# Layer 2 by one level of Strassen (7 products), remainder tokens as one 512-token group, batch 0 by head halves, loads on GpSimd's queue, and an issue order from a list scheduler

## The chip, the cores and the metric

One core of one Trainium2 chip. The metric is the device time of one execution in microseconds (us), the median of several; the span of a profile is a little shorter than that time. Engines are named as in the profile: PE is TensorE (matmul), DVE is VectorE, ACT is ScalarE, POOL is GpSimd, SP is SyncE, which here only issues DMAs.

## The reference, cut to what matters

```python
# q, k, v: (8 batches, 8 heads, 576 tokens, 64), float32
def attn(q, k, v):
    phi = lambda x: concat([relu(x) * cos_w, relu(x) * sin_w], axis=-1)   # 128 features
    q_p, k_p = phi(q), phi(k)
    kv  = einsum('bhsf,bhsd->bhfd', k_p, v)
    z   = sum(k_p, axis=2)
    num = einsum('bhsf,bhfd->bhsd', q_p, kv)
    den = einsum('bhsf,bhf->bhs', q_p, z)[..., None] + 1e-6
    return num / den

x   = attn(q, k, v).transpose(0, 2, 1, 3).reshape(4608, 512)
h   = x @ w_in                 # layer 1: 512 -> 2048
out = (h * cos(h)) @ w_out     # layer 2: 2048 -> 512
```

A batch has 576 = 4 x 128 + 64 tokens. Four tiles of 128 are its own; the 64 left over, the remainder, pair with the 64 of the next batch into a fifth tile.

## The kernel before

The parts that the change and the argument touch. All loads of q, k, v and all transposing DMAs are issued by SP, in one queue:

```python
    def load(b, name, after=None):
        ...
        m, n = raw[name], b % 2                      # one f32 buffer each for q, k, v
        five, four = tokens(srcs[name][b])
        nc.sync.dma_start(out=blocks(m, n), in_=five)
        nc.sync.dma_start(out=blocks(m, 1 - n)[:, :, 0:NT, :], in_=four)

    def q_trans_dma(b):                              # batches 2 to 7; PE transposes 0 and 1
        nc.sync.dma_start_transpose(
            out=qTs[b].rearrange("f t h p -> f (t h) p"),
            in_=qps[b].rearrange("p t h g d -> p (t h g d)"))

    def num(b, t):
        ... # matmuls of qT with kvz, then on DVE: den, reciprocal, x16 = N * rec
            if b >= NPE:
                nc.sync.dma_start_transpose(out=x_dst(b, t), in_=x16s[(b, t)])

    def moe1(b, j, s0=0, s1=SM):                     # layer 1: 4 matmuls of 512 columns
        ...
        gate(gts[b][:, j, s0:s1], M1)                # ACT: sin(h + pi/2); DVE: product

    def moe2(key, t, gsl, j0=0, j1=NJT):             # layer 2: 16 matmuls of 512 columns
        ...
            nc.tensor.matmul(
                M2, lhsT=gts[key][:, j, gsl], rhs=w_out_sb[:, j, :],
                start=(j == 0), stop=(j == NJT - 1))
```

The next batch's attention is spread by hand over the layers of the present one.

Of the kernel before, what the change touches and what calls it, by code (L numbers as in the profile page):

```python
# [13 lines left out]
F16 = mybir.dt.float16  # L14


@with_exitstack
def kernel(
# [31 lines left out]
    for n in range(2):  # L50
# [11 lines left out]
        tc.tile_pool(name="ppool", bufs=8, space=bass.MemoryType.PSUM))  # L62
# [5 lines left out]
    V1 = [cpool.tile([P, NT + 1, H, D1], F16, name=f"V1_{n}") for n in range(2)]  # L68

    srcs = {"k": k, "v": v, "q": q}  # L70
    raw = {nm: cpool.tile([P, H, NT + 1, D], F32, name=f"{nm}m") for nm in srcs}
    kvzs, kps, qps, qTs, x16s, xts, gts, m2s, osts = {}, {}, {}, {}, {}, {}, {}, {}, {}
    ALLP = slice(0, P)


    late = []

    def flush():
        todo, late[:] = list(late), []
        for f in todo:  # L80
            f()

    def tokens(ap):

        return (ap[..., 0:S5, :].rearrange("h (p t) d -> p h t d", t=NT + 1),
                ap[..., S5:S, :].rearrange("h (p t) d -> p h t d", t=NT))

    def load(b, name, after=None):
        if b >= B:
            return  # L90
        m, n = raw[name], b % 2
        if after is not None:
            nc.gpsimd.tensor_copy(out=m[0:2, 0, 0, 0:1], in_=after)
        five, four = tokens(srcs[name][b])
        nc.sync.dma_start(out=blocks(m, n), in_=five)
        nc.sync.dma_start(out=blocks(m, 1 - n)[:, :, 0:NT, :], in_=four)

    def feat(b, name, t, g, act):


        dst = (kps if name == "k" else qps)[b][:, t, :, g, :]
        src, sc = raw[name][:, :, t, :], CS[:, b % 2, g, t:t + 1]
        if act:
            nc.scalar.activation(out=dst, in_=src, func=AF.Relu, scale=sc)  # L104
        else:
            nc.vector.tensor_scalar(  # L106
                out=dst, in0=src, scalar1=0.0, scalar2=sc, op0=ALU.max, op1=ALU.mult)

    def val(b, t, act):
        dst, src = V1[b % 2][:, t, :, 0:D], raw["v"][:, :, t, :]  # L110
        if act:
            nc.scalar.activation(out=dst, in_=src, func=AF.Copy)  # L112
        else:
            nc.vector.tensor_copy(out=dst, in_=src)  # L114

    def kv_group(b, hb):
        KV = ppool.tile([P, HB, D1], F32, name=f"KV{b}_{hb}", tag="ps")
        for hh in range(HB):
            h = hb * HB + hh
            for t in range(NT + 1):  # L120
                nc.tensor.matmul(  # L121
                    KV[:, hh, :], lhsT=kps[b][:, t, h].rearrange("p g d -> p (g d)"),
                    rhs=V1[b % 2][:, t, h, :], start=(t == 0), stop=(t == NT))
        nc.scalar.activation(
            out=kvzs[b][:, hb * HB:(hb + 1) * HB, :], in_=KV, func=AF.Copy)

    def q_trans_dma(b):

        nc.sync.dma_start_transpose(
            out=qTs[b].rearrange("f t h p -> f (t h) p"),  # L130
            in_=qps[b].rearrange("p t h g d -> p (t h g d)"))

    def q_trans(b, t):
        QP = ppool.tile([P, H, P], F16, name=f"QP{b}_{t}", tag="ps")
        for h in range(H):
            nc.tensor.matmul(  # L136
                QP[:, h, :], lhsT=qps[b][:, t, h].rearrange("p g d -> p (g d)"),
                rhs=IDENT, is_transpose=True)
        nc.scalar.activation(out=qTs[b][:, t], in_=QP, func=AF.Copy)  # L139

    def num(b, t):

        parts = [b - 1, b] if t == NT else [b]
        N = [ppool.tile([P, HB, D1], F32, name=f"NUM{b}_{t}_{hb}", tag="ps")
             for hb in range(2)]
        for hb in range(2):
            for hh in range(HB):
                h = hb * HB + hh
                for n, p in enumerate(parts):
                    nc.tensor.matmul(  # L150
                        N[hb][:, hh, :], lhsT=qTs[p][:, t, h, :], rhs=kvzs[p][:, h, :],
                        start=(n == 0), stop=(n == len(parts) - 1))

        def ratio():
            den = apool.tile([P, H], F32, name=f"den{b}_{t}", tag="den")
            for hb in range(2):
                nc.vector.tensor_scalar_add(
                    out=den[:, hb * HB:(hb + 1) * HB], in0=N[hb][:, :, D], scalar1=1e-6)
            rec = apool.tile([P, H], F32, name=f"rec{b}_{t}", tag="rec")
            nc.vector.reciprocal(out=rec, in_=den)  # L160
            x16 = apool.tile([P, H, D], F16, name=f"x16{b}_{t}", tag="x16", bufs=4)
            for hb in range(2):
                sl = slice(hb * HB, (hb + 1) * HB)
                nc.vector.tensor_tensor(
                    out=x16[:, sl, :], in0=N[hb][:, :, 0:D],
                    in1=rec[:, sl].unsqueeze(2).broadcast_to((P, HB, D)), op=ALU.mult)
            x16s[(b, t)] = x16.rearrange("p h d -> p (h d)")
            if b >= NPE:
                nc.sync.dma_start_transpose(out=x_dst(b, t), in_=x16s[(b, t)])
        late.append(ratio)  # L170

    def x_dst(b, t):
        if t < NT:
            return xts[b][:, :, t * P:(t + 1) * P]
        xts[("r", b // 2)] = apool.tile([P, NCT, P], F16, name=f"xTr{b}", tag="xTr")
        return xts[("r", b // 2)]

    def x_trans(b, t):
        XP = ppool.tile([P, NCT, P], F16, name=f"XP{b}_{t}", tag="ps")
        for c in range(NCT):  # L180
            nc.tensor.matmul(
                XP[:, c, :], lhsT=x16s[(b, t)][:, c * P:(c + 1) * P], rhs=IDENT,
                is_transpose=True)
        nc.scalar.activation(out=x_dst(b, t), in_=XP, func=AF.Copy)

    def attention_tiles(b):
        kps[b] = apool.tile([P, NT + 1, H, 2, D], F16, name=f"kp{b}", tag="kp", bufs=1)
        qps[b] = apool.tile([P, NT + 1, H, 2, D], F16, name=f"qp{b}", tag="qp", bufs=1)
        kvzs[b] = apool.tile([P, H, D1], F16, name=f"kvz{b}", tag="kvz", bufs=3)
        qTs[b] = apool.tile([P, NT + 1, H, P], F16, name=f"qT{b}", tag="qT")  # L190
        xts[b] = apool.tile([P, NCT, SM], F16, name=f"xT{b}", tag="xT")

    def gate(dst, M1):

        n = M1.shape[-1]
        ch = apool.tile([P, SM], F32, name="ch", tag="ch", bufs=4)
        nc.scalar.activation(out=ch[:, 0:n], in_=M1, func=AF.Sin, bias=PIH, scale=1.0)  # L197
        flush()
        late.append(lambda: nc.vector.tensor_tensor(
            out=dst, in0=M1, in1=ch[:, 0:n], op=ALU.mult))  # L200

    def moe1(b, j, s0=0, s1=SM):
        if b not in gts:
            gts[b] = gpool.tile([P, NJT, SM], F16, name=f"g{b}", tag="g")
        M1 = ppool.tile([P, s1 - s0], F32, name="M1", tag="ps")
        for c in range(NCT):
            nc.tensor.matmul(  # L207
                M1, lhsT=w_in_sb[:, c, j * P:(j + 1) * P], rhs=xts[b][:, c, s0:s1],
                start=(c == 0), stop=(c == NCT - 1))
        gate(gts[b][:, j, s0:s1], M1)  # L210

    def moe1_rem(pr, jg):
        if jg == 0:
            gts[("r", pr)] = gpool.tile([P, NJT, P], F16, name=f"gr{pr}", tag="gr")
        M1 = ppool.tile([P, 4, P], F32, name="M1", tag="ps")
        for jj in range(4):
            j = jg * 4 + jj
            for c in range(NCT):
                nc.tensor.matmul(  # L219
                    M1[:, jj, :], lhsT=w_in_sb[:, c, j * P:(j + 1) * P],  # L220
                    rhs=xts[("r", pr)][:, c, :],
                    start=(c == 0), stop=(c == NCT - 1))
        gate(gts[("r", pr)][:, jg * 4:(jg + 1) * 4, :].rearrange("p j s -> p (j s)"),
             M1.rearrange("p j s -> p (j s)"))

    def moe2(key, t, gsl, j0=0, j1=NJT):
        if j0 == 0:
            m2s[(key, t)] = ppool.tile([P, Dm], F32, name="M2", tag="ps")
        M2 = m2s[(key, t)]
        for j in range(j0, j1):  # L230
            if j == 1:
                flush()
            nc.tensor.matmul(  # L233
                M2, lhsT=gts[key][:, j, gsl], rhs=w_out_sb[:, j, :],
                start=(j == 0), stop=(j == NJT - 1))
        return M2

# [5 lines left out]
    def moe2_main(b, t, j0=0, j1=NJT):  # L243
        if t == 0 and j0 == 0:
            flush()
        M2 = moe2(b, t, slice(t * P, (t + 1) * P), j0, j1)
        if j1 < NJT:
            return
# [27 lines left out]
    def spread(main, side):  # L276
# [7 lines left out]
        for _, f in side:  # L284
            f()
# [175 lines left out]
```

## Time and profile before

| | before |
|---|---|
| time, median of 3 before the prediction (5 in all) | 313.51 us (314.14) |
| span of the profile | 311.2 us |
| PE / DVE / ACT / POOL busy | 92% / 59% / 58% / 9% |
| layer 2 of batch 0 begins | 38.8 us |
| DMA engines' share in 64 to 225 us | 0.85 |

From the chain that ended last, in order of time (start us, us, what; x16 means 16 instructions):

```profile
88.93 3.19 DMA xT_819<-x_3_1232
92.12 0.14 issue
92.25 1.86 PE M_1262 L207 x4
94.12 1.57 PE M_1270 L207 x4
95.69 0.86 PE M_1281 L207 x4
...
303.34 3.47 PE M_3707 L233 x16
```

A layer-2 tile of 16 matmuls takes 3.45 to 3.47 us, a layer-1 unit of 4 takes 0.86. From 88.93 the chain waited 3.19 us for a transposing DMA, and the two units after it took 1.86 and 1.57 us: the granted clock was 0.50 from 92.1 to 95.4 us.

PE's waits for transposing DMAs in this kernel are these two, 3.7 us in all (engine, who waited, for whom: us in total, times, longest us):

```profile
PE M_1262 L207 <- DMA xT_819<-x_3_1232: 3.2, 1, 3.2
PE M_1655 L207 <- DMA xT_1258<-x_3_1575: 0.5, 1, 0.5
```

### The profile page before, as it was taken

The page shows a single profiled execution, that of the slowest core. Times are in us where ns is not written, and L with a number is a line of the kernel's source. Part 1 is how long each engine was busy: PE and PEld are TensorE (multiplying, and loading weights), DVE is VectorE, ACT ScalarE, POOL GpSimd, SP SyncE. Part 2 cuts the span into 40 slices and gives each one's busy share as a digit, 9 for nine tenths or more (in the row PEclk, how much of TensorE's full clock was granted, in tenths as well). Part 3 has the DMA queues.
Part 4 walks back from the last instruction along what each step waited for, and adds up shares of the span by engine and source line. Part 5 has one row for each costly group of instructions (what it writes and reads, how often), then busy time and mean ns, then how long its engine had stood idle before and what let it go on. Part 6 is the DMA issues. An engine that isn't in the chain of part 4 may idle for free.

```text
span 311.2 us, 5548 instructions
## 1 busy us (share of the span) xinstructions
PE 285.3 (92%) x2124; PEld 153.9 (49%) x2124; DVE 185.1 (59%) x457; ACT 179.2 (58%) x301; POOL 27.6 (9%) x55
## 2 busy tenths in 40 slices
PE   0389999799959999999999999999999999999994
PEld 0377447445724454445744554446644554447441
DVE  2677790699737665766937565966757581565000
ACT  2679787399407852875557732884458543566111
POOL 0810001100010101010011101010001101010110
PEclk9999999999998999999999999999999999999999
DMA  7999989409990999279934999099937541010121
GB/s 227 305 208 206 326 275 351 155 2 171 334 256 0 140 332 253 90 145 309 275 101 83 239 368 192 1 206 316 211 97 139 135 86 68 1 67 2 67 103 67
DMA packets 78587, 53.76 MB, mean 173 GB/s; under 512 B 47456, under 2 KB 76128, under 8 KB 78560
## 3 DMA queue, kind: packets, MB, share of 16 engines
q1 hardware_dynamic: 71264, 40.51, 54.8%
q0 software_dynamic: 6848, 12.59, 15.5%
q8 instruction: 17, 0.28, 0.4%
q10 hardware_dynamic: 448, 0.31, 0.3%
q14 instruction: 10, 0.08, 0.1%
HBM read 36.74 MB, written 9.44 MB: 148 GB/s over the span
## 4 chain that ended last, share of the span: by engine, by line
PE 79%; ACT 7%; DVE 6%; DMA 5%; issue 2%; SPq 0%; ACTq 0%; DVEq 0%
DMA vm<-in_v_dram 2%; DMA xT_1258<-x_3_1575 1%; ACT ch L197 1%; ACT qT_108 L139 1%; PE M_3707 L233 1%; PE M_3064 L233 1%; PE M_2210 L233 1%; PE M_1726 L233 1%; PE M_2584 L233 1%; PE M_699 L233 1%; PE M_3645 L233 1%; PE M_3489 L233 1%; PE M_2931 L233 1%; PE M_2486 L233 1%; PE M_2140 L233 1%
## 5 line engine op out<-in xcount | busy, mean ns | idle before, releaser
L207 PEld LDWEIGHTS <-w_in_sb 128*128 128x128 f16 x536 | 51.2, 98 | 60.8 <-issue 8.2
L265 POOL DMA_DIRECT2D out_dram<-ost x14 | 7.4, 530 | 211.8 <-ACT ost L259 211.8
L219 PEld LDWEIGHTS <-w_in_sb 128*128 128x128 f16 x256 | 14.7, 98 | 0.9
L121 PE MATMUL KV_0_125<-V_0_71,kp_105 128*128 128x65 f16 x20 | 1.6, 240 | 11.6 <-DVE V_0_71 L114 11.1
L257 DVE COPY ost<-M_3707 128x256 f32<-128x256 f32 x1 | 0.4, 424 | 19.7 <-ACT ost L255 19.7
L112 ACT ACTIVATE V_0_71<-vm 128x512 f16<-128x512 f32 x17 | 10.7, 635 | 0.1
L233 PEld LDWEIGHTS <-g_3357 128*128 128x128 f16 x64 | 6.3, 98 | 7.5
L233 PEld LDWEIGHTS <-g_2957 128*128 128x128 f16 x64 | 6.2, 98 | 7.3
L233 PEld LDWEIGHTS <-g_1654 128*128 128x128 f16 x64 | 6.2, 98 | 7.3
L233 PEld LDWEIGHTS <-g_2512 128*128 128x128 f16 x64 | 6.2, 98 | 7.3
L233 PEld LDWEIGHTS <-g_1261 128*128 128x128 f16 x64 | 6.2, 98 | 7.1
L233 PEld LDWEIGHTS <-g_2099 128*128 128x128 f16 x64 | 6.2, 98 | 7.1
L233 PEld LDWEIGHTS <-g_322 128*128 128x128 f16 x64 | 6.1, 98 | 6.8
L233 PEld LDWEIGHTS <-g_822 128*128 128x128 f16 x64 | 6.0, 98 | 6.9
L112 ACT ACTIVATE V_1_72<-vm 128x512 f16<-128x512 f32 x15 | 9.2, 627 | 0.0
L121 PEld LDWEIGHTS <-kp_105 128*128 128x128 f16 x40 | 2.3, 130 | 11.7 <-ACT kp_105 L104 11.1
L266 POOL DMA_DIRECT2D out_dram<-ost x14 | 7.6, 543 | 0.3 <-issue 0.3
L274 POOL DMA_DIRECT2D out_dram<-ostr x8 | 4.3, 545 | 37.0 <-ACT ostr L271 37.0
L104 ACT ACTIVATE kp_105<-km,CS 128x512 f16<-128x512 f32 x5 | 3.2, 709 | 4.6 <-DMA km<-in_k_dram 4.6
L106 DVE TENSOR_SCALAR kp_105<-km,CS 128x512 f16<-128x512 f32 x5 | 2.1, 483 | 4.7 <-DMA km<-in_k_dram 4.7
L136 PEld LDWEIGHTS <-qp_106 128*128 128x128 f16 x40 | 4.1, 146 | 1.4 <-ACT qp_106 L104 1.2
L207 PE MATMUL M_1262<-xT_819,w_in_sb 128*128 128x512 f16 x4 | 1.9, 620 | 3.2 <-DMA xT_819<-x_3_1232 3.2
(924 smaller groups left out, 752.0 us busy)
## 6 DMA issues: line engine op xcount, KB each, us to landing
out_dram<-ost POOLq DMA_DIRECT2D x28, 256.0 KB, 2.8
km<-in_k_dram SPq DMA_DIRECT2D x8, 640.0 KB, 9.1
vm<-in_v_dram SPq DMA_DIRECT2D x8, 640.0 KB, 8.3
qm<-in_q_dram SPq DMA_DIRECT2D x8, 640.0 KB, 6.7
km<-in_k_dram SPq DMA_DIRECT2D x8, 512.0 KB, 9.6
vm<-in_v_dram SPq DMA_DIRECT2D x8, 512.0 KB, 9.1
qm<-in_q_dram SPq DMA_DIRECT2D x8, 512.0 KB, 7.9
w_in_sb<-in_moe_w_in_dram POOLq DMA_DIRECT2D x4, 512.0 KB, 8.9
```

Source lines behind the costliest of these rows:

```text
L104: nc.scalar.activation(out=dst, in_=src, func=AF.Relu, scale=sc)
L112: nc.scalar.activation(out=dst, in_=src, func=AF.Copy)
L121: nc.tensor.matmul(KV[:, hh, :], lhsT=kps[b][:, t, h].rearrange("p g d -> p (g d)"), rhs=V1[b % 2][:, t, h, :], start=(t == 0), stop=(t == ...
L136: nc.tensor.matmul(QP[:, h, :], lhsT=qps[b][:, t, h].rearrange("p g d -> p (g d)"), rhs=IDENT, is_transpose=True)
L139: nc.scalar.activation(out=qTs[b][:, t], in_=QP, func=AF.Copy)
L197: nc.scalar.activation(out=ch[:, 0:n], in_=M1, func=AF.Sin, bias=PIH, scale=1.0)
L207: nc.tensor.matmul(M1, lhsT=w_in_sb[:, c, j * P:(j + 1) * P], rhs=xts[b][:, c, s0:s1], start=(c == 0), stop=(c == NCT - 1))
L219: nc.tensor.matmul(M1[:, jj, :], lhsT=w_in_sb[:, c, j * P:(j + 1) * P], rhs=xts[("r", pr)][:, c, :], start=(c == 0), stop=(c == NCT - 1))
L233: nc.tensor.matmul(M2, lhsT=gts[key][:, j, gsl], rhs=w_out_sb[:, j, :], start=(j == 0), stop=(j == NJT - 1))
L265: eng.dma_start(out=five[:, t - 1:t + 1, :], in_=blocks(ost, n))
L266: eng.dma_start(out=four[:, t - 1:t + 1, :], in_=blocks(ost, 1 - n))
L274: nc.gpsimd.dma_start(out=five[:, NT, :], in_=blocks(ost, n))
```

## The change

Its intent is fewer PE cycles. One level of Strassen does the layer-2 product of a 512-token group with 7 products of half size instead of 8, so 112 matmuls of 256 columns in place of 64 of 512; it pays with sums on DVE. Its buffers take SBUF, so the transposed q (`qT`) goes from two buffers to one. All remainder tiles wait for a common group `"r"` at the end. Batch 0 is loaded and worked on by head halves. A list scheduler fixes the order on every engine at build time from assumed durations. And loads of batches 2 to 7 move from SP's queue to POOL's, while the transpose of q becomes five smaller DMAs. The core of a long diff:

```diff
+class Plan:                    # list scheduler: durations, rings of buffers, priorities
+    SEM, EPS = 0.08, 0.1
+    ...
-        tc.tile_pool(name="ppool", bufs=8, space=bass.MemoryType.PSUM))
+        tc.tile_pool(name="ppool", bufs=4, space=bass.MemoryType.PSUM))  # 4 layer 1, 2 layer 2, 1 pair
+    def qT_tiles(b):
+        qTs[b] = apool.tile([P, NT, H, P], F16, name=f"qT{b}", tag="qT", bufs=1)
+    def q_trans_dma(b, t):
         nc.sync.dma_start_transpose(
-            out=qTs[b].rearrange("f t h p -> f (t h) p"),
-            in_=qps[b].rearrange("p t h g d -> p (t h g d)"))
+            out=qT(b, t), in_=qps[b][:, t].rearrange("p h g d -> p (h g d)"))
+                    load(b, name, nc.sync if b < 2 else nc.gpsimd)
+                li = op({SQ: 1.35} if b < 2 else {"G": 2.1}, ...)
+                land[(b, name)] = op({DQ: 3.3}, (b, i), deps=[li], lat=LAND)       # LAND = 2.0
+                qtd[((0, 1), t)] = op({DQ: 1.0}, (b, 0), deps=[i], lat=LAND, rel=[sl["qp"]])
+    def sums(g, c, n):          # DVE, f16, 128x1024 each, 8 per group
+        out, in0, in1, op = ((s1, a21, a22, ALU.add), (s2, s1, a11, ALU.subtract),
+                             (a21, a11, a21, ALU.subtract), (a12, a12, s2, ALU.subtract))[n]
+    def prod(g, n, c):          # 7 products into three PSUM banks X, Y, Z
+        for i in range(2):
+            for j in range(c * HJ // 2, (c + 1) * HJ // 2):
+                nc.tensor.matmul(
+                    ps[(g, bank)][:, i, :], lhsT=lhs[:, j, i * P:(i + 1) * P], rhs=rhs[:, j], ...)
+    GO = [0, 1, 2, 3, 4, 5, 6, "r", 7]          # group 0 plain, the other eight by Strassen
 ...
```

## The prediction

> **What bounds the kernel now.** TensorE. The page gives PE 285.3 us busy of a 311.2 us span (92%), DVE 185.1 (59%), ACT 179.2 (58%); PE is 79% of the chain that ended last. Rates from that chain: a 16-matmul layer-2 tile takes 3.45 us (216 ns per 512-column matmul), a 4-matmul 256-column unit 0.44 us (109 ns each), 16 remainder matmuls of 128 columns 0.89 us (56 ns), a KV half 0.60 us (30 ns). [...] So weight loads don't bind at 256 columns, which Strassen needs.
> At these rates PE's work is 124.4 (layer 1) + 124.4 (layer 2) + 19 (KV, NUM) + 6.4 (transposes) = 274 us. The other 37: about 20 before layer 2 begins at 38.95 us (first KV matmul at 11.1, cold clock, attention of batch 0); 12.7 in the middle, of which two transposing DMAs that land late behind a batch load (chain: 3.19 and 4.62 us; after the first, two units take 1.86 and 1.57 us instead of 0.86) and the gaps at 58 to 66 us; 4.4 in the tail.
>
> **What changes, costed.**
> 1. Strassen for 8 of 9 token groups: 896 matmuls of 256 columns at 109 ns = 98.0, plus the plain group 13.8: 111.8 us for 124.4. Gain 12.6, all critical. Remainders at 512 columns: 0.4.
> 2. DVE pays: 64 sums of f16 128x1024 and 40 adds from PSUM. [...]I estimate 0.69 us a sum, like the 512-element f32 gate (692 ns here); no such sum is in the trace. 44 + 28 + 5 (weight sums) = +77 us, less 29 for q features moved to ACT (60 x 0.48) and a little for merged ratios: DVE about 230 us, near 80%. ACT: +43 (q features), -12 (fewer evictions): about 205, 70%. Per group 23 to 27 us of DVE against 28 of PE: close, not binding on average.
> 3. Start: half-head loads let batch 0 begin at about 7 us, warm-up matmuls spare the cold clock (transposes at 131 ns instead of 56). But all of q, k, v must land (about 14 us), then the weights. Layer 1 of batch 0 ends 4 to 5 us earlier.
> 4. Middle: loads leave the queue of the transposes, features run ahead: about 7 of the 12.7 us go.
> 5. New costs: chained products on few banks, each waiting for an eviction; the last group's layer 2 alone; a larger last store: +2.5.
>
> **Sum.** 313.5 - 13 - 4.5 - 7 + 2.5 = 291.5 us. I say 291, 80% range 284 to 301. Faster by over 2%: 0.92; within 2%: 0.06; slower: 0.02.
>
> **If right, the profile shows:** PE work down by 12 us; layer-2 units of 16 matmuls at 1.74 us; sums near 0.69 us; DVE near 80%; layer 2 begins at about 34 us; no wait for a transposing DMA above 1 us; PE over 90% busy from 40 us on; a tail of 4 to 6 us.
> **Wrong if:** [...]the chain shows DVE adds or gates ahead of matmuls throughout (an order planned with durations that the chip does not keep); 256-column matmuls exceed 115 ns; loads issued by POOL come late. Better than 284 if start and middle close entirely.

That weight loads do not bind at 256 columns rests on its rates alone (216, 109 and 56 ns for 512, 256 and 128 columns, with as many weight loads as matmuls, x2124); in the changed kernel a 256-column matmul takes 109 ns too (16 in 1.75 us). The 0.69 us a sum, and with it the 44 and 5 us in DVE's load, were the author's estimate by likeness to the gate, not shown by the trace before; measured in the changed kernel are 0.68 us a sum and 1.22 us a weight sum. Its "cold clock" is in that trace a duration: 8 transposes took 1.05 us at 15.3 us and 0.45 at 47.6. After the warm-up matmuls of the changed kernel 20 KV matmuls took 0.73 us (1.11 before); then, from 17.2 to 24.0 us, the granted clock was 0.50.

## More of the kernel before

In SP's queue the transpose of q comes first and the next loads stand behind it; every second batch also carries the layers of a remainder tile:

```python
                side += [(5.5, lambda: q_trans_dma(b)), (5.6, lambda: load(b + 1, "q")),
                         (6.4, lambda: load(b + 1, "v")), (11.6, lambda: load(b + 1, "k")),
                         (14.0, lambda: kv_group(b, 0)), (14.8, lambda: kv_group(b, 1))]
                side += [(15.7 + 1.2 * t, lambda t=t: num(b, t))
                         for t in range(NT + b % 2)]
```

From the page of the kernel before: busy us of each engine with its share of the span and its instructions; then rows of 40 equal slices of the span, each digit the busy share in tenths (PEclk: the clock granted to PE, in tenths of full speed).

```profile
PE 285.3 (92%) x2124; PEld 153.9 (49%) x2124; DVE 185.1 (59%) x457; ACT 179.2 (58%) x301; POOL 27.6 (9%) x55
...
PE   0389999799959999999999999999999999999994
...
PEclk9999999999998999999999999999999999999999
DMA  7999989409990999279934999099937541010121
```

PE is busy nearly everywhere after the first three slices and keeps its clock.

How SP's queue is filled, from the timeline of SP (start us, us, what):

```profile
69.90 6.19 SPq L129 DMA_TRANSPOSE qT_818<-qp_816  x1
76.14 0.61 SPq L95 DMA_DIRECT2D qm<-in_q_dram  x1
76.85 0.60 SPq L96 DMA_DIRECT2D qm<-in_q_dram  x1
77.56 0.60 SPq L95 DMA_DIRECT2D vm<-in_v_dram  x1
```

The transpose of q goes in at 69.90, the loads from 76.14 on: behind it, in the same queue. It landed at 77.9 us, the first of these loads at 81.1.

## The result

The changed kernel takes 331.67 us (median of 5, 330.32 to 339.16) against 314.14 us (median of 5, 313.12 to 315.04). The ratio of the fast runs is 1.0558, 95% interval 1.0506 to 1.061: slower by 5.6%. Ratios here are the mean time of one kernel's fast runs over that of the other's of the same rounds, so not quite the ratio of the medians. Two of the five runs of the changed kernel, the profiled one among them, are over 1.5% longer than its fastest and count as slow. Nothing below rests on the difference between its slow and fast runs; its clock is low in the fast ones as well (0.919 to 0.940). But the span of the profiled run, 336.4 us, is 6.5 to 7.8 us longer than those of the fast ones (328.6 to 329.9), so the waits read from it may be that much larger than theirs.

From the page of the changed kernel, in answer to the lines of before:

```profile
PE 287.0 (85%) x2504; PEld 201.6 (60%) x2504; DVE 228.5 (68%) x437; ACT 194.3 (58%) x337; POOL 65.9 (20%) x112
...
PE   8479998798549967991199977999999999999994
...
PEclk9959999799959995998589997999999999999998
...
DMA  6699999999995996789969998480340110110113
```

From slice 11 to slice 25 PE has holes and a clock below full speed; from slice 28 on it is full and the DMA row nearly empty. PE's waits, from the view of waits. In the names of the changed kernel, M is layer 1, N the product of q's features with KV, TP a transpose by PE, and PX, PY, PZ the products of Strassen:

```profile
PE N L225 <- DMA qT<-qp: 23.2, 5, 14.0
PE M L269 <- DMA xT<-x: 7.9, 1, 7.9
PE N L225 <- DVE x L238: 4.4, 4, 1.6
```

31.1 us of waiting for transposing DMAs, in six places, against 3.7 us in two before. The four longest (2.9 us and more) are also paid for in clock: the granted clock was 0.50 from 92.3 to 102.6, 126.5 to 133.3, 157.2 to 170.8 and 205.0 to 208.4 us, during or after them; after the two of 1.6 and 0.2 us, at 199.3 and 222.3, it was 1.00. The chain of the changed kernel around the wait of 7.9 us, and around the longest wait:

```profile
85.39 11.55 DMA xT<-x
96.93 0.14 issue
97.07 3.57 PE M L269 x8
...
148.33 18.48 DMA qT<-qp
166.81 0.05 issue
166.86 0.62 PE N L225 x8
```

Eight layer-1 matmuls take 3.57 us at 97.07 where two units at a granted clock of 1.00 take 1.73. And one transpose of q needs 18.48 us. What else is under way then is on POOL's timeline and on SP's:

```profile
147.38 0.69 POOL L169 DMA_DIRECT2D km<-in_k_dram  x1 [5.73 <-ACT kp L176]
148.06 0.69 POOL L170 DMA_DIRECT2D km<-in_k_dram  x1
148.74 0.69 POOL L169 DMA_DIRECT2D vm<-in_v_dram  x1
149.43 0.69 POOL L170 DMA_DIRECT2D vm<-in_v_dram  x1
```

```profile
148.33 19.23 SPq L259 DMA_TRANSPOSE qT<-qp  x4
```

In the same two microseconds POOL puts 2.36 MB of loads into its own queue and SP begins to put in four transposes; SP alone needs 19.23 us until it is rid of them. The chain shows that these transposes, like those before the wait of 4.5 us at 127.96, were released by the last features from ACT (at 148.28 and 117.44 us), not by the single `qT` buffer. Before, the loads stood behind the transpose. The windows of the two kernels over the attention stages, first before and then after, columns as their own heading has them (us, PE, PEld, DVE, ACT, POOL busy with instruction counts, PEclk, DMA share, GB/s):

```profile
core 0: us, PE busy (x) PEld busy (x) DVE busy (x) ACT busy (x) POOL busy (x), PEclk, DMA share, GB/s
64.00:225.00 161.00, 155.59 (x1190) 82.27 (x1189) 111.55 (x279) 97.24 (x168) 9.71 (x19) 0.99 0.85 194
```

```profile
64.00:225.00 161.00, 128.21 (x1195) 87.96 (x1194) 103.57 (x199) 111.93 (x195) 37.93 (x60) 0.89 0.95 194
225.00:336.40 111.40, 106.77 (x778) 73.69 (x775) 79.19 (x128) 39.41 (x66) 10.68 (x20) 0.99 0.17 58
```

The same 194 GB/s pass in both, but the DMA share (it adds up the times of packets, delays within a packet included) rises from 0.85 to 0.95, PE's busy time falls by 27 us and its clock to 0.89. After 225 us DMA has almost nothing to do (0.17): the layers of the gathered remainders lie there, while before they lay among the attention stages and gave DMA time.

What went as foreseen: 16 matmuls of a Strassen unit take 1.75 us, the sums 0.68 us at the median, DVE is busy for 228.5 us, the tail after the last matmul is 4.6 us. The start did not: layer 2 begins at 39.3 us, not at 34.

### The profile page after: what moved, and what is told of

It is laid out like the page before. It is cut to its first block, busy times and chain, and to the rows that moved or that the text cites. A ratio compares the mean times of both kernels' runs of the same rounds, so it can differ in the third digit from the quotient of the medians.

```text
span 336.4 us, 6418 instructions
## 1 busy us (share of the span) xinstructions
PE 287.0 (85%) x2504; PEld 201.6 (60%) x2504; DVE 228.5 (68%) x437; ACT 194.3 (58%) x337; POOL 65.9 (20%) x112
## 3 DMA queue, kind: packets, MB, share of 16 engines
q10 hardware_dynamic: 992, 1.22, 1.1%
## 4 chain that ended last, share of the span: by engine, by line
PE 72%; DMA 18%; DVE 5%; ACT 2%; issue 1%; ACTq 0%; DVEq 0%
PE M L269 35%; DMA qT<-qp 13%; PE PY L327 11%; PE PX L327 8%; PE PZ L327 7%; PE M L366 4%; DMA xT<-x 3%; PE N L225 3%; PE KV L216 2%; DMA qm<-in_q_dram 2%; PE TP L253 2%; DVE x L238 2%; ACT qp L176 1%; DVE rec L234 1%; ACT kp L176 1%
## 5 line engine op out<-in xcount | busy, mean ns | idle before, releaser
L276 ACT ACTIVATE ch<-M 128x512 f32<-128x512 f32 x144 | 85.5, 596 | 97.3 <-PE M L269 96.5
L269 PE MATMUL M<-xT,w_in_sb 128*128 128x512 f16 (+1 forms) x640 | 128.6, 351 | 8.0 <-DMA xT<-x 7.9
L282 DVE TENSOR_TENSOR g<-M,ch 128x512 f16<-128x512 f32 x128 | 86.4, 688 | 44.1 <-ACT ch L276 43.1
L327 PEld LDWEIGHTS <-g 128*128 128x128 f16 x560 | 54.9, 99 | 12.0 <-issue 0.6
L176 ACT ACTIVATE qp<-qm,CS 128x512 f16<-128x512 f32 (+1 forms) x71 | 46.5, 690 | 2.5 <-DMA qm<-in_q_dram 2.5
L176 ACT ACTIVATE kp<-km,CS 128x512 f16<-128x512 f32 (+1 forms) x63 | 40.1, 691 | 6.9 <-DMA km<-in_k_dram 6.9
L225 PEld LDWEIGHTS <-qT 128*128 128x128 f16 x256 | 12.6, 103 | 34.1 <-DMA qT<-qp 25.5
L327 PE MATMUL PY<-WT,g 128*128 128x256 f16 x224 | 28.4, 282 | 0.0
L327 PE MATMUL PX<-w_out_sb,g 128*128 128x256 f16 x224 | 27.2, 272 | 0.0
L238 DVE TENSOR_TENSOR x<-N,rec 128x512 f16<-128x512 f32 (+1 forms) x40 | 25.5, 638 | 1.4
L327 PEld LDWEIGHTS <-s 128*128 128x128 f16 x224 | 21.4, 98 | 5.7 <-DVE s L299 1.2
```

The lines of the kernel that those rows point to most:

```text
L176: nc.scalar.activation(out=dst, in_=src, func=AF.Relu, scale=sc)
L225: nc.tensor.matmul(tile_[:, n, hh, :], lhsT=qT(p, t)[:, h, :], rhs=kvzs[p][:, h, :], start=(i == 0), stop=(i == len(parts) - 1))
L238: nc.vector.tensor_tensor(out=dst, in0=tile_[:, :, :, 0:D], in1=rec.unsqueeze(3).broadcast_to((P, nb, HB, D)), op=ALU.mult)
L269: nc.tensor.matmul(ps[key][:, n, :], lhsT=w_in_sb[:, c, j * P:(j + 1) * P], rhs=x[:, c, s0:s1], start=(c == 0 and n == 0), stop=(c == NCT ...
L276: nc.scalar.activation(out=ps[("ch", key)], in_=ps[key].rearrange("p j s -> p (j s)"), func=AF.Sin, bias=math.pi / 2.0, scale=1.0)
L282: nc.vector.tensor_tensor(out=dst, in0=m, in1=ps[("ch", key)].rearrange("p (j s) -> p j s", s=m.shape[2]), op=ALU.mult)
```

## The experiments

Four theories for where the 40 us between 291 and 331.7 went:

- **A, mixed queues.** Loads on a queue of their own share the DMA engines with the transposes and stretch them.
- **B, capacity.** Transposes, loads and stores together fill the DMA engines in the attention stages, whatever the queue.
- **C, order.** Transposes are issued too late: one `qT` buffer, and a plan made with durations that are too short.
- **D, Strassen itself.** Its sums and its chain of products stall PE.

The runs below have 4 timings each (the last has 6), beside the kernel before on the same chip. The runs were made on several chips, so differences of medians between runs are good to a few us (the kernel before had medians of 313.46 to 314.94 us on them, and the times of e1 alone lie 6 us apart); where it matters, the mean of the fast runs stands beside them (331.1 us for the changed kernel). The profiles of e1 and e10 are of slow runs. One build never got to a chip: the changed kernel with two `qT` buffers again, which the build refused because its last pool no longer fitted. So the single buffer could not be tried by itself, nor was the split of q's transpose into five; e6 below keeps both and has few of the waits.

### e1: loads back on SyncE's queue

```diff
-                    load(b, name, nc.sync if b < 2 else nc.gpsimd)
+                    load(b, name, nc.sync)
```

> The loads of batches 2 to 7 go back to the queue of SyncE, in the places of the same plan; nothing else changes. Theory A (mixed queues: the loads, in large packets on a queue of their own, share the DMA engines with the transposing DMAs and stretch them): transposes keep their turn, PE's waits for transposing DMAs fall from 31 us to under 10, the time falls to 300 +- 6 us. Theory B (capacity: transposes, loads and stores together fill the DMA engines in the attention stages, whatever the queue): within 2% of the changed kernel's 331. Theory C (transposes issued too late, one qT buffer and a plan with short durations): within 2% of 331 as well. Theory D (Strassen itself: its adds and its chained products stall PE): no change.

Measured: 313.53 us (309.19 to 315.35), ratio to before 0.9927 (0.9855 to 0.9999), so within 2% of it. The plan was not touched, only the queue: 18 us came back by the medians, 20 by the fast runs (331.1 - 311.2; e1 has only two, 4 us apart). The view of waits of e1, then the landing times of the q transposes in the changed kernel and in e1 (from issue to landing):

```profile
PE N L225 <- DMA qT<-qp: 10.3, 4, 3.5
PE N L225 <- DVE x L238: 4.4, 4, 1.6
```

```profile
DMA to landing us min/median/max: 3.1/5.4/18.5
```

```profile
DMA to landing us min/median/max: 3.0/4.3/9.0
```

Theory A is right in kind, and its size came out lower than expected: 313.5, not 300 +- 6, and 10.3 us of waits for q transposes are left.

### e5: nearly no load traffic (wrong result)

```diff
-                    load(b, name, nc.sync if b < 2 else nc.gpsimd)
+                    load(b, name, nc.sync if b < 2 else nc.gpsimd, ALLH if b < 2 else slice(0, 1))
```

> Loads of batches 2 to 7 fetch one head of eight, so nearly all load traffic of the middle is gone, with the order untouched; the result is wrong on purpose. Theories A and B: DMA waits of PE fall below 5 us and the time to 295 +- 6 us. Theory C: the transposes are late all the same, over 320. Theory D: over 325.

Measured: 298.82 us (298.31 to 299.64). PE's waits for DMAs are 0.4 us in all; the line of that wait, and how q transposes land:

```profile
PE N L225 <- DMA qT<-qp: 0.4, 1, 0.4
DMA to landing us min/median/max: 3.0/3.3/4.9
```

Of the 40.7 us between prediction and result, 32.9 (331.7 - 298.8) depend on the load traffic. The order of the changed kernel is not at fault as long as DMAs are quick; theory D cannot be the main cause.

### e2: q transposed by TensorE for all batches

```diff
-        if b > 1:
+        if b > B:
             for t in T1:
                 i = op({SQ: 1.35}, (b - 1, 0, t), lambda t=t: q_trans_dma(b, t), ...
```

> The q features of all batches are transposed by TensorE, as batches 0 and 1 are; 27 to 30 transposing DMAs of q are gone. 240 more PE transposes at 56 ns are 13.4 us. Theories A, B, C: DMA waits nearly vanish, 300 to 310 us. Theory D: the 13.4 us come on top, 340 or more.

Measured: 315.66 us (ratio 1.0078, 1.0033 to 1.0123), and PE's list of waits has no q transpose and no x transpose in it. 315.7 less the 13.4 us of added PE work is 302.3, near e5. The measured time is above the 300 to 310 us that theories A, B and C had foreseen, and far below D's 340. It is the same answer from the other side: take the q transposes off the DMA engines, leave all loads on POOL's queue, and the waits are gone. It does not tell A from B.

### e3: all of the change but Strassen

```diff
-            layer2(GO[p - 1], lambda i, p=p, q=pos2: (1, p + 1, q[i]))
+            layer2_plain(GO[p - 1], lambda t, n, p=p, q=pos2: (1, p + 1, q[2 * t + n]))
 ...  # no sums, no weight sums; layer2_plain made to take a group
```

> Everything of the change but Strassen: layer 2 of all groups by plain 512-column matmuls (12.6 us more PE work), no sums, no combining adds. Theory D: faster than the changed kernel, 315 or less. Theory A: 331 + 5 to 12. Theory B: the attention stages are held by DMA and don't lengthen, only the groups after them do, so 331 + 2 to 6.

Measured: 334.45 us (331.01 to 342.21), ratio to before 1.0634. In the changed kernel Strassen is worth about 334.5 - 331.7 = 2.8 us of its 12.6 (2.2 by the fast runs); the intervals of the two ratios overlap, so this is hardly clear of noise. By the prediction's arithmetic PE's work grew by 12.6, but in the attention stages the DMAs set the pace, so most of the extra work fell into waits: those for transposing DMAs are 22.6 us in e3 (15.8 for x, 6.8 for q), 31.1 in the changed kernel. That is the size that theory B foresaw (2 to 6). Theory D is out: without Strassen the kernel is not faster.

### e7: the same with little load traffic (wrong)

The edits of e3 and of e5 together:

```diff
+            layer2_plain(GO[p - 1], ...)          # as in e3
+                    load(b, name, nc.sync if b < 2 else nc.gpsimd, ALLH if b < 2 else slice(0, 1))
```

> e3 (plain layer 2) with the small loads of e5; wrong on purpose. What Strassen is worth once DMA holds nothing: if its PE saving is as costed, 12.6 us slower than e5's 298.8, so 311 +- 3. If its sums, adds and chained products eat much of it, under 306.

Measured: 305.03 us (304.57 to 305.76) against e5's 298.82. Freed of DMA, Strassen is worth 6.2 us by the medians and 4.8 by the ratios to the kernel before (0.9688 - 0.9536, of 314): at most half of the PE time that it saves. About 1.5 us of the rest are lost before layer 2 begins (40.2 us in e5, 38.7 in e7). Windows of e5 and of e7 over the stage where its sums begin (columns as above):

```profile
40.00:100.00 60.00, 55.08 (x579) 40.77 (x578) 48.15 (x98) 51.58 (x89) 18.88 (x32) 0.94 0.64 148
```

```profile
40.00:100.00 60.00, 58.31 (x568) 37.83 (x567) 42.23 (x90) 53.11 (x93) 21.37 (x37) 1.00 0.65 152
```

With Strassen, DVE has 5.9 us more to do there, PE waits 4.2 us for x tiles of DVE instead of 1.0 and loses 3.2 us of busy time, and its clock falls to 0.94, which I estimate at about 3 us more (0.06 x 55). From 100 us on both keep PE nearly full.

### e8: loads on ScalarE's queue

```diff
-                    load(b, name, nc.sync if b < 2 else nc.gpsimd)
+                    load(b, name, nc.sync if b < 2 else nc.scalar)
```

> The loads of batches 2 to 7 on ScalarE's queue: a second queue beside the transposes, as in the changed kernel, but with packets of 1024 and 1280 bytes instead of 4096 and 5120. If the harm comes from the size of the packets[...], the time lies near e1's, 308 to 318 (less where ScalarE itself isn't held up), and transposes of q land in under 5 us at the median and 10 at most. If any second queue does the same harm, 325 or more and landings up to 15 us.

Measured: 320.82 us (317.6 to 323.07), between e1 and the changed kernel, landings of q 3.0 / 7.9 / 11.6 us (least, median, longest). Neither expectation holds whole: by the medians a second queue costs about 7 us by itself, and POOL's queue, with its large packets, about 11 more. The packet records of the traces show the sizes:

```text
                      loads of batches 2 to 7: bytes, median ns of one     transposes: bytes, median ns
kernel before (SP)    1,024 B 47 ns; 1,280 B 55 ns                         256 B, 18 ns
changed kernel (POOL) 4,096 B 172 ns; 5,120 B 220 ns                       256 B, 18 ns
e1 (SP), e8 (ACT)     1,024 B, 1,280 B; in e1 46 ns, 55 ns                 256 B, 18 ns
```

So beside POOL's queue the 256-byte packets of a transpose are in flight with loads' packets of up to 5,120 bytes; beside ACT's, of up to 1,280; and in SP's one queue a transpose that was issued first was done first (in the kernel before, 1.9 to 4.7 us before the first load behind it). The times of the three runs and their longest landings (18.5, 11.6 and 9.0 us) have this order, the medians do not (5.4, 7.9, 4.3). ScalarE, which issues in e8, may have been held up too, so the split into 7 and 11 us is rough, and that the size of the packets makes it is argued, not shown. How the engines choose between queues was not shown either.

Size cannot be all of it. During the longest wait of the changed kernel, from 152 to 166 us, the packets fill the engines' time (share 1.16), and yet only 133 GB/s pass; just before, from 150 to 152 us, it was 364. Single packets of 5,120 bytes take up to 3.2 us there, against 0.22 at the median, and some of 256 bytes 2.4 us. So in this window, with both kinds of traffic in flight, the engines also moved less. Why this is so stays open.

### e6: e1, with a plan that knows the DMAs

```diff
-                li = op({SQ: 1.35} if b < 2 else {"G": 2.1}, (b - 1, 1, i), issue, ...
+                li = op({SQ: 1.35}, (b - 1, 1, i), issue, ...
-                qtd[((0, 1), t)] = op({DQ: 1.0}, (b, 0), deps=[i], lat=LAND, rel=[sl["qp"]])
+                qtd[((0, 1), t)] = op({DQ: 1.75}, (b, 0), deps=[i], lat=0.5, rel=[sl["qp"]])
-                    i = op({SQ: 0.65}, (b - 1, 0.5, t), ...            # issue of an x transpose
+                    i = op({SQ: 1.25}, (b - 1, 0.5, t), ...
-                    x_done[b][(hbs, t)] = op({DQ: 0.6}, (b, -1), deps=[i], lat=LAND, rel=[xs])
+                    x_done[b][(hbs, t)] = op({DQ: 0.9}, (b, -1), deps=[i], lat=0.5, rel=[xs])
```

> e1 (loads on SyncE's queue) with the plan told of it, and given the durations that the runs show for the DMAs: 1.75 us instead of 1.0 for a q transpose, 1.25 us instead of 0.65 to issue an x transpose, 0.9 instead of 0.6 to move it, less landing time. Theory A with C (what is left of e1's 14 us over the run with little load traffic is order): 300 to 305 us, PE's waits for DMAs under 4 us. Theory B (what is left is DMA capacity, 0.90 of the DMA engines' time in 64 to 225 us): within 1.5% of e1, 307 to 315.

Measured: 305.70 us (303.09 to 307.27), ratio to before 0.9699 (0.9631 to 0.9767). 7.8 us less than e1 (5.7 by the fast runs), and faster than the kernel before. The time lies just outside both foreseen ranges, but PE's waits for transposing DMAs are down to 2.7 us, as the first expectation said. So order (C) was a part of it. The wait that is left, then the windows of e1 and of e6 (columns as above):

```profile
PE M L269 <- DMA xT<-x: 2.7, 1, 2.7
64.00:225.00 161.00, 149.10 (x1390) 104.64 (x1388) 124.98 (x239) 121.75 (x212) 21.77 (x36) 0.96 0.90 207
64.00:225.00 161.00, 153.85 (x1430) 107.45 (x1428) 137.99 (x260) 119.22 (x207) 20.77 (x35) 0.99 0.94 208
```

The DMA share in 64 to 225 us is 0.94 all the same, and was 0.90 in e1, so capacity (B) was not what held e1. One thing is new here; a line of DVE's timeline and one of POOL's:

```profile
146.11 3.15 DVE L299 TENSOR_TENSOR s<-g 128x1024 f16<-128x1024 f16 x1
```

```profile
145.87 2.84 POOL L160 CAST V<-vm 128x512 f16<-128x512 f32 x5
```

A sum of 0.68 us took 3.15 while POOL copied V, and PE waited 2.77 us for it.

### e9: first loads in order on one queue

```diff
     nc.scalar.dma_start(out=CS, in_=cs_dr.ap())
-    piece("k", 0, 0, nc.scalar)
+    nc.scalar.dma_start(out=IDENT, in_=ident_dr.ap())
+    piece("k", 0, 0, nc.sync)
     piece("q", 0, 1, nc.sync)
-    piece("q", 0, 0, nc.scalar)
-    nc.scalar.dma_start(out=IDENT, in_=ident_dr.ap())
+    piece("q", 0, 0, nc.sync)
```

> e1 with all six first half loads in order on SyncE's queue, and the identity ahead of them on ScalarE's. If the start failed because two queues shared the engines and the first halves landed late (k at 8.5, q at 10.2 us): the first k half is used at about 6.5, the first q half at about 8 us, layer 2 begins 1.5 to 2 us earlier than in e1, the time falls as much. If VectorE and ScalarE hold the start whatever the loads do (90% and 87% busy from 10 to 20 us): less than 0.7 us.

Measured: 311.20 us (310.18 to 312.92) against e1's 313.53 (309.19 to 315.35): the ranges overlap, so the time alone is inconclusive. Where DVE first uses a half of k, in the changed kernel and in e9:

```profile
8.54 1.67 DVE L178 TENSOR_SCALAR kp<-km,CS 128x256 f16<-128x256 f32 x6 [6.56 <-DMA km<-in_k_dram]
```

```profile
5.79 1.67 DVE L178 TENSOR_SCALAR kp<-km,CS 128x256 f16<-128x256 f32 x6 [3.82 <-DMA km<-in_k_dram]
```

The kernel before uses the whole of k at 7.26 us. So in the changed kernel half of k came later than the whole had come before: its two pieces went into two queues and shared the engines with everything behind them (up to 15 us the packets of SP's queue took 57.7% of the engines' time, those of ACT's 15.7%, and ACT's piece of k landed after 6.9 us). In order, it comes at 5.79. But of these 2.8 us only 1.2 reach the start of layer 2 (38.90 against e1's 40.12). This lies between the two expectations (1.5 to 2 us, and under 0.7): the order of the loads is a part, and DVE and ACT, which the second one named, may hold the rest.

### e10, e12, e13: three repairs that made it worse

e10 moves the weight sums to POOL:

```diff
-        nc.vector.tensor_tensor(out=WT[:, n], in0=x, in1=y, op=ALU.subtract)
+        nc.gpsimd.tensor_tensor(out=WT[:, n], in0=x, in1=y, op=ALU.subtract)
-        wsum.append(op({"V": 1.25}, (1.5, n), ...
+        wsum.append(op({"G": 4.5}, (1.5, n), ...
```

e12 takes the V copies off POOL:

```diff
-                    {"V": 0.45, "A": 0.6, "G": 1.9} if b == 1 else {"A": 0.6, "G": 1.9},
+                    {"V": 0.45, "A": 0.6} if b == 1 else {"A": 0.6},
```

Both start from e6. e13 is e6 with both and with e9's start.

> e6 with the four sums of weight quadrants on GpSimd instead of VectorE, planned anew. Strassen was worth 6 us of its 12.6 with little load traffic (e7 against e5); PE lost the rest at 54 to 100 us, waiting for VectorE's x tiles and then running on the cold clock. If VectorE's load there, of which the weight sums are 4.9 us, is the cause: the waits of NUM for x fall below 1.5 us and the time falls 2 to 4 us from e6's 305.7. If not: within 1 us[...].

> e6 with no V copies on GpSimd (ScalarE takes them). In e6 one sum on VectorE took 3.15 us, beside a run of five GpSimd copies of 2.84 us, and PE waited 2.8 us for it. If the copies block sums: no sum above 1.0 us, and 1 to 3 us less than e6. If the long sum has another cause: one is seen here too, the time within 1 us of e6.

> e6 with all three: weight sums on GpSimd, V copies on ScalarE, first half loads in order on SyncE's queue (e9). If they add up: 298 to 302 us, layer 2 begins at 38.5 to 39 us. It should beat the kernel before by 4 to 5%.

Measured: 310.61 (308.73 to 315.75), 308.09 (307.55 to 308.61) and 314.96 us (314.04 to 318.17), all slower than e6 by their medians (e12's by 2.4 us, on another chip, its interval of ratios just touching e6's). In e10, a line of POOL's timeline, one of DVE's and one of PE's:

```profile
49.53 4.08 POOL L306 TENSOR_TENSOR WT<-w_out_sb 128x2048 f16<-128x2048 f16 x1
```

```profile
49.09 9.99 DVE L178 TENSOR_SCALAR qp<-qm,CS 128x512 f16<-128x512 f32 x4
```

```profile
58.04 3.57 PE L253 MATMUL TP<-IDENT,qp 128*128 128x128 f16 x32 [8.89 <-DVE qp L178]
```

Four features that take 0.48 us each took 9.99 us while two weight sums of POOL ran (4.08 and 4.05 us), and PE waited 8.89 us. As in e6, instructions of DVE beside long ones of POOL took several times as long. It does not hold for all of them: at 39.4 to 41.9 us in e10, beside another weight sum of POOL (38.84 to 42.91), three gates of DVE took their 0.69 us. Which instructions hold each other up, and how, was not shown.

In e12 no sum lasts over 0.69 us, as expected if the copies blocked sums; but the new plan ran into a wait of 7.1 us for an x transpose at 101.6 us. Removing a cause of 2.8 us moved the order and brought another of 7.1. e13 began layer 2 at 37.9 us and then lost it all to the same weight sums, with 11.5 us of waiting for features. So what the long sum costs in e6 was not confirmed by a time; only that it goes with the copies was, by the durations.

### e14: e6 with e9's start

```diff
 # e6, and the edit of e9 to piece("k", 0, 0, ...) and piece("q", 0, 0, ...): nc.scalar -> nc.sync
```

> e6 with only the first half loads in order on SyncE's queue (e9's start); weight sums and V copies as in e6. e9 began layer 2 1.2 us earlier than e1 and was 2 us faster, with overlapping spreads. If the start adds up: layer 2 begins at about 38.5 instead of 39.8 us, 303 to 305 us, 3 to 3.5% under the kernel before. If it is noise, or the new plan falls on other stalls as in e12: 305 to 308.

Measured: 303.82 us (302.32 to 304.84), ratio to before 0.9674 (0.9637 to 0.971). Layer 2 begins at 37.5 us instead of 39.8. This version is correct and beats both kernels: 3.3% under the kernel before, 8.4% under the changed one (303.82 / 331.67). From e6 the time alone does not tell it: 305.70 us, and the intervals of the ratios overlap.

## Why the prediction was wrong, point by point

It said 291 us and 0.92 for faster; the kernel was 5.6% slower.

1. **Middle: this is the step that failed.** "Loads leave the queue of the transposes, features run ahead: about 7 of the 12.7 us go." It took the move to another queue for a relief, because the trace of before shows two transposes that are late behind loads. The runs show the reverse. Nor had DMAs cost 7 us there: before, PE waited 3.7 us in all for transposing DMAs and lost about 1.7 to the clock after the first (1.86 + 1.57 - 2 x 0.86); the 4.62 us that the prediction read in the chain for the second cost PE 0.5. In one queue, each q transpose landed before any of the loads behind it (in the kernel before, by 1.9 to 4.7 us); from another queue the loads are in flight beside the transposes, in larger packets when that queue is POOL's (4,096 and 5,120 bytes for 1,024 and 1,280). Instead of winning 7 us there, the kernel lost 32.9 against e5, the run in which loads hold nothing: 18.2 us through the queue (e1) and 7.8 through an order planned with too short DMA durations (e6). By the fast runs these are 19.9 and 5.7 us. The remaining 6.9, from e6 to e5, is not settled: e5 also frees the DMA engines, whose share e6 leaves at 0.94. In the prediction's list of what might go wrong, "loads issued by POOL come late" was near, but it was the transposes that came late; so was "an order planned with durations that the chip does not keep", though it had DVE in mind and not the DMAs.
2. **What was not asked: how full the DMA engines are.** The page of before shows the DMA row near full in the attention stages (0.85 in 64 to 225 us). The change shortens PE's part of these stages and moves the remainders' layers to the end, where the DMA share is 0.17. The waits then fell on DMAs, and the prediction costed only PE, DVE and ACT. A full share alone does not slow the kernel, as e6 shows with 0.94. The gathering of the remainders was not undone in a run, so its part of this is argued, not shown.
3. **Strassen: PE arithmetic right, effect too large.** 12.6 us "all critical" is what PE saves; units took 1.75 us, and sums 0.68 us, as estimated by likeness to the gates' 0.69. Its effect was about 2.8 us in the changed kernel (e3), for most of its saving went into waits for DMAs there (31.1 us against e3's 22.6), and 4.8 to 6.2 with DMA out of the way (e7, e5): where the sums begin, DVE comes late (PE waits 4.2 us for x tiles instead of 1.0) and PE pays again in clock (0.94 instead of 1.00 from 40 to 100 us).
4. **Start: -4.5 was predicted, +0.5 came** (layer 2 at 39.3 for 38.8). Half loads did not come at 7 us: k's first half at 8.5, q's at 10.3, as two queues shared the engines (e9, with one queue: 5.8 and 7.9). And even with loads in order not all of it came, probably because of DVE and ACT (90% and 87% busy from 10 to 20 us in the changed kernel); e14 gets 1.3 us against the kernel before.
5. **DVE and ACT load: right.** 228.5 and 194.3 us busy for 230 and 205 foreseen; "close, not binding on average" held after 100 us with DMA out of the way (e5: PE 124.53 of 125 us busy from 100 to 225).
6. **Tail: right,** 4.6 us in the foreseen 4 to 6.

The terms for e5, where loads hold nothing, nearly close, as an estimate that takes the 7 us of the middle as won: 291 + 5 to 6 (start not won, layer 2 at 40.2 for 34) + 6.4 (Strassen's half) - 2.5 (already allowed for new costs) = about 300 to 301, measured 298.8.

## What to carry to other kernels

Before cutting the work of the busiest engine, read how full the next resource is in the stage in question, DMA engines included, and ask what the shorter stage demands of it. Moving transfers to another queue did not get them out of one another's way here: the small-packet transfers that PE waits for did better ahead of bulk loads in the same queue than beside them (longest landing of a q transpose 9.0 us in e1, 18.5 in the changed kernel). A fixed order is as good as the durations that it was planned with; those of DMAs must be measured under the load that they will meet (a q transpose landed after 3.3 us at the median in e5, 4.3 in e1, 5.4 in the changed kernel), and each repair changes the order, so it must be run.
